# A fifth gate/up weight pair in the storage of a later table: ten f-tiles on token block 0 before block 1 in a fused SSM + GLU kernel

## The chip, the cores and the metric

One core of a Trainium2 chip runs the whole kernel. The metric is the device time of one execution in microseconds (us), read from repeated executions; each ratio compares kernels on one chip, but the chips differ between groups of experiments (1 to 3 with 5; 4 with 6 to 8; 9 and 10; 11 and 12). All comparisons are between executions in the fast state; the only one marked slow (at a granted clock of 0.993) is left out and named where it fell. In experiments 4, 9 and 10 some executions that count as fast have a clock of 0.993 to 0.997; where that matters it is said. A profile is one execution.

Names: PE does the matmuls, DVE and ACT are the vector and scalar engines, POOL is GpSimd and here mostly issues loads, SP (SyncE) issues the transposing transfers. A *token block* is 512 tokens. An *f-tile* is 128 columns of the gate and up weights; a *pair* is the weights of two f-tiles (576 KB). A *slot* is 12 f-tiles on two token blocks, followed by a *down stage*.

## The reference

```python
xn = layernorm(x)                        # x: 1 x 2048 x 576
out = x + A(xn) + B(xn)
def A(x):                                # diagonal complex state-space model, 576 states
    dt = exp(log_dt); Lam_bar = exp(dt * Lam)
    Bu = einsum("bld,pd->blp", x, ((Lam_bar - 1) / Lam)[:, None] * Bmat)
    h[t] = Lam_bar * h[t-1] + Bu[:, t]
    return 2 * einsum("blp,dp->bld", h, Cmat).real + x * Dskip
def B(x):                                # gated MLP, 576 -> 4608 -> 576
    return (sigmoid(x @ w_gate) * (x @ w_up)) @ w_down
```

## The kernel before

The instruction order on every engine is the order of emission. The first loads, all but the first tokens from POOL:

```python
def load_wgu(key, eng_g, eng_u):
    ...
    w = wpool.tile([P, NH, FP * P], BF16, name="wgu", bufs=4)      # four pairs fit
    ...
for pr in range(2):
    load_wgu((0, pr), nc.gpsimd, nc.gpsimd)
for tt in range(TT_B, 2 * TT_B):
    load_x(tt, nc.gpsimd, "hst")
dskip_rows = consts.tile([P, D], BF16, name="dskip_rows")
nc.gpsimd.dma_start(dskip_rows[:], A_Dskip.partition_broadcast(P))
for pr in range(2, 4):
    load_wgu((0, pr), nc.gpsimd, nc.gpsimd)
```

Block 1's tokens are normalised on DVE and transposed by four SP transfers (`xT<-xn`); then DVE adds the skip term for eight token tiles (`ln_resid`, which reads `dskip_rows`). A gate/up group is 18 matmuls, two evictions by ACT (`sT`, `uT`) and one product on DVE (`hT`):

```python
def evac(self):
    ...
    nc.scalar.activation(sT[:], self.ps[:, 0, :], ACT.Sigmoid)
    nc.scalar.copy(uT[:], self.ps[:, 1, :])
    h = hpool.tile([P, TB], BF16, name="hT", bufs=2 * FC)
    nc.vector.tensor_mul(h[:], sT[:], uT[:])
    ...
    bg.step(...)      # gives time credit to queued background work (skip terms, SSM chain)
```

Slot 0's order, and the loads of its down weights:

```python
order = [(f, 0) for f in range(2, 8)] + [(f, 1) for f in range(0, 8)]     # (0,0) and (1,0) come first
order += [(f, nb) for nb in range(2) for f in range(8, 12)]
...
if g.slot == 0:
    if n_used >= 16:
        prefetch_wd(n_pairs)          # six loads of down weights
...
side_loads.extend([load_consts] + bt_loads)     # nine small SSM constants, then transposes of B
```

Of the kernel before, what the change touches and what calls it, by code (L numbers as in the profile page):

```python
# [13 lines left out]
BF16 = mybir.dt.bfloat16  # L14
# [52 lines left out]
def kernel(  # L67
# [17 lines left out]
    nc = tc.nc  # L85
    P = 128
# [8 lines left out]
    TB = 512  # L95
# [7 lines left out]
    NU = PT + 1  # L103
# [3 lines left out]
    NH = D // H  # L107
    FQ = 4
    FP = 2
# [9 lines left out]
    consts = ctx.enter_context(tc.tile_pool(name="consts", bufs=1))  # L119
    wpool = ctx.enter_context(tc.tile_pool(name="wpool", bufs=1))  # L120
# [13 lines left out]
    def load_x(tt, eng, tag=None):  # L134
        if tag is None:
            xt = lnp.tile([P, D], BF16, name="xt", bufs=8)
        else:
            xt = hpool.tile([P, D], BF16, name="xt0", tag=tag, bufs=10)
        eng.dma_start(xt[:], x[tt * P:(tt + 1) * P, :])
        xts[tt] = xt  # L140
# [4 lines left out]

    def load_wgu(key, eng_g, eng_u):
        f0 = (key[0] % NC * (FC // FP) + key[1]) * FP * P
        w = wpool.tile([P, NH, FP * P], BF16, name="wgu", bufs=4)
        fs = slice(f0, f0 + FP * P)
        for (eng, rows, src) in ((eng_g, slice(0, H), B_w_gate), (eng_u, slice(H, P), B_w_up)):  # L150
            eng.dma_start(w[rows, :, :], src[:, fs].rearrange("(c p) f -> p c f", p=H))  # L151
        wgu_t[key] = w
# [12 lines left out]
        load_wgu((0, pr), nc.gpsimd, nc.gpsimd)  # L165
    for tt in range(TT_B, 2 * TT_B):
        load_x(tt, nc.gpsimd, "hst")
    dskip_rows = consts.tile([P, D], BF16, name="dskip_rows")
    nc.gpsimd.dma_start(dskip_rows[:], A_Dskip.partition_broadcast(P))
    for pr in range(2, 4):  # L170
        load_wgu((0, pr), nc.gpsimd, nc.gpsimd)

    eps_t = consts.tile([P, 1], FP32, name="eps_t")
    nc.vector.memset(eps_t[:], 1e-5)
# [132 lines left out]
    qim = consts.tile([P, NU], FP32, name="qim")  # L307
    nqre = consts.tile([P, NU], FP32, name="nqre")
    c512, s512 = sc4[:, 3, :], sc4[:, 2, :]
    T1 = consts.tile([P, NU, TB], BF16, name="T1")  # L310
    T2 = consts.tile([P, NU, TB], BF16, name="T2")
    C2 = consts.tile([P, NU, TB], BF16, name="C2")
    S2 = consts.tile([P, NU, TB], BF16, name="S2")
# [62 lines left out]
        nc.vector.tensor_scalar(s512[:, PT:NU], s512[:, PT:NU], sg_pm[:], -1.0, ALU.mult, ALU.mult)  # L376

    def tables(pt, part):
        sb_, cb_ = sc_tab[(pt, 0)], sc_tab[(pt, 1)]
        col = slice(pt, pt + 1)  # L380
        if part == 0:
            t = ssmp.tile([P, TB], FP32, name="ttab", tag="bure", bufs=2)
            nc.vector.tensor_scalar_mul(t[:], sb_[:], qim[:, col])
            nc.vector.scalar_tensor_tensor(T1[:, pt, :], cb_[:], qre[:, col], t[:], ALU.mult, ALU.add)
            return
        t2 = ssmp.tile([P, TB], FP32, name="ttab2", tag="buim", bufs=2)
        nc.vector.tensor_scalar_mul(t2[:], sb_[:], nqre[:, col])
        if pt < PT:
            nc.vector.scalar_tensor_tensor(T2[:, pt, :], cb_[:], qim[:, col], t2[:], ALU.mult, ALU.add)
            nc.vector.tensor_scalar_mul(C2[:, pt, :], cb_[:], 2.0)  # L390
        else:
            nc.vector.scalar_tensor_tensor(t2[:], cb_[:], qim[:, col], t2[:], ALU.mult, ALU.add)
            nc.vector.tensor_scalar(T2[:, pt, :], t2[:], sg_pm[:], -1.0, ALU.mult, ALU.mult)
            nc.vector.tensor_scalar(C2[:, pt, :], cb_[:], sg_pm[:], 2.0, ALU.mult, ALU.mult)
        nc.vector.tensor_scalar_mul(S2[:, pt, :], sb_[:], -2.0)
# [14 lines left out]
    def ssm_w(nb, pt, part):  # L410
        bre, bim = bu[(nb, pt)]
        t1, t2 = T1[:, pt, :], T2[:, pt, :]
        if part == 0:
# [59 lines left out]
    bg = Background()  # L473
# [63 lines left out]
    def emit(g):  # L537
        g.open()
        g.mms()
        g.evac()  # L540
# [85 lines left out]
    def want_bu(i):  # L626
        if i < len(chain):
            bu_wanted.append(chain[i])
# [25 lines left out]
    n_slots = NSB * NC  # L654
    n_pairs = FC // FP
    all_pairs = [(s, p) for s in range(n_slots) for p in range(n_pairs)]
    wgu_next = [4]
    wd_next = [0]
    pairs_done = [0]

    def prefetch_wgu(n):
        while wgu_next[0] < min(n, len(all_pairs)):
            load_wgu(all_pairs[wgu_next[0]], nc.gpsimd, nc.gpsimd)
            wgu_next[0] += 1

    def prefetch_wd(n):
        while wd_next[0] < min(n, len(all_pairs)):
            load_wd(all_pairs[wd_next[0]])
            wd_next[0] += 1
# [3 lines left out]
    def used(g):  # L673
        if not isinstance(g, GateUp):
            return
        key = (g.slot, g.f // FP)
        uses[key] = uses.get(key, 0) + 1
        if uses[key] == FP * NB_SB:
            pairs_done[0] += 1
            prefetch_wgu(pairs_done[0] + 4)  # L680

        n_used = sum(v for k, v in uses.items() if k[0] == g.slot)
        if g.slot == 0:
            if n_used >= 16:
                prefetch_wd(n_pairs)
        elif n_used % 3 == 0:
            prefetch_wd(g.slot * n_pairs + min(n_used // 3, n_pairs))

    def between_steps():

        if 1 in ssm_done and 1 not in c_done and glu_done[0]:
            for tl in range(TT_B):
                d_step(TT_B + tl, c_terms(1, tl), True)
                acc_free[0] = TT_B + tl + 1
            c_done.add(1)

    def flush_bu():
        if bu_wanted:
            emit(StateIn(*bu_wanted.popleft()))

    def catch_up(nb):

        while nb not in ssm_done:
            flush_bu()
            bg.step(5.0)

    side_loads = deque()

    def run_groups(groups):
        for i, g in enumerate(groups):  # L710
            flush_bu()
            emit(g)
            used(g)
            if side_loads and i % 3 == 2:
                side_loads.popleft()()
            between_steps()

# [68 lines left out]
    for g in start_groups:  # L786
        g.evac()
        used(g)
        bg.step(4.5)

    def catch_up_ln(nb):
        while nb not in ln_done:
            bg.step(5.0)

    for sb in range(NSB):
        b0 = sb * NB_SB
        for c in range(NC):
            slot = sb * NC + c
            if slot == 0:
                order = [(f, 0) for f in range(2, 8)] + [(f, 1) for f in range(0, 8)]  # L800
                order += [(f, nb) for nb in range(2) for f in range(8, 12)]
            else:
                order = [(f, b0 + nbl) for fq in range(0, FC, 4) for nbl in range(NB_SB) for f in range(fq, fq + 4)]
            if slot == 1:
                side_loads.extend(ct_loads)
                for i in range(len(chain)):
                    queue_ssm(i)
                want_bu(0)
                want_bu(1)
            if slot == 2:  # L810
                queue_ln(2, 0)
                queue_ln(2, 1)
            if slot == 0:
                run_groups([GateUp(slot, f, nb) for (f, nb) in order[:6]])
                catch_up_ln(1)
                order = order[6:]
                side_loads.extend([load_consts] + bt_loads)
            run_groups([GateUp(slot, f, nb) for (f, nb) in order])
            if slot == 0:
                split_bt()  # L820
                bg.add(0.0, sines)
                bg.gap()
                bg.add(2.9, per_state_q)
                for pt in range(NU):
                    bg.add(1.2, lambda pt=pt: tables(pt, 0))
                    bg.add(2.1, lambda pt=pt: tables(pt, 1))
            if slot == 2:
                catch_up(0)
                catch_up_ln(2)
                queue_ln(3, 0)  # L830
                queue_ln(2, 2)
                queue_ln(3, 2)
            for tt in range(NB_SB * TT_B):
                nbl, tl = divmod(tt, TT_B)
                nb = b0 + nbl
                final = c == NC - 1 and (nb != 1 or 1 in ssm_done)
                if final:
                    catch_up(nb)
                terms = [(hT[(f, nb)][:, tl * P:(tl + 1) * P], wd_t[(slot, f // FP)][:, f % FP, :]) for f in range(FC)]
                if final:  # L840
                    terms += c_terms(nb, tl)
                d_step(sb * NB_SB * TT_B + tt, terms, final, last=slot == n_slots - 1 and tt == NB_SB * TT_B - 1)
                if slot == 2 and final:
                    acc_free[0] = tt + 1
                if slot == 2 and tt == TT_B - 1:
                    c_done.add(0)
                if slot == 2 and tt == NB_SB * TT_B - 1:
                    glu_done[0] = True
                    if final:
                        c_done.add(1)  # L850
                between_steps()
# [30 lines left out]
```

## Time and profile before

| | before |
|---|---|
| median of the runs given at first | 509.85 us |
| span of the profiled execution | 508.4 us |
| PE busy | 500.6 us |
| block 1's transposes landed (issue of the last plus its time to landing) | 27.4 us |
| first down stage on PE begins | 58.71 us |

The prediction shows the totals, PE's waits and the gap. In the timeline of the kernel before, columns are start, duration, engine, line, operation, tiles, count, and in brackets the idle time before with what ended it.

```profile
7.40 0.54 POOL L169 DMA_DIRECT2D dskip_rows<-in_A_Dskip_dram  x1 [0.67 <-DMA wgu<-in_B_w_gate_dram]
...
58.71 11.57 PE L562 MATMUL pd<-wd,hT 128*128 128x288 bf16 x93
```

The skip row is asked for at 7.40, ahead of pairs 2 and 3, and POOL's issue itself waits for earlier loads. This view is cut at its end; in the prediction's chain all 192 matmuls of the first down stage are one piece.

### The profile page before, as it was taken

To read this page: it belongs to the slowest core of one execution; us is meant where nothing else is said; L and a number is where in the kernel's file an instruction comes from. 1 tells how busy PE (TensorE), PEld (TensorE's weight loads), DVE (VectorE), ACT (ScalarE), POOL (GpSimd) and SP (SyncE) were. 2 spreads that over 40 slices of the span, in tenths; PEclk is the share of its full clock that TensorE was granted. 3 is DMA by queue.
4 is the path that set the end of the run, shared out by engine and by line. 5 is a ranking of instruction groups with operands and counts; after the bars stand their busy time and mean duration, and the time that the engine had idled before them with its cause. 6 is when DMAs were issued, how large, how long until landed. Compare 5 with 4: busy or idle time off the path is not lost.

```text
span 508.4 us, 10667 instructions
## 1 busy us (share of the span) xinstructions
PE 500.6 (98%) x4536; PEld 292.6 (58%) x4536; DVE 323.5 (64%) x703; ACT 204.6 (40%) x368; POOL 96.6 (19%) x143
## 2 busy tenths in 40 slices
PE   8989999999999999999999999999999999999996
PEld 5445676444477444467764444774444774446775
DVE  6964999977888587868688667786675222221111
ACT  4757642556500756530016655005655005553000
POOL 6147430133110043110001231100431001300000
PEclk9999999999999999999999999999999999999999
DMA  8997997075220098342340662200753201600001
GB/s 208 172 170 143 235 194 125 2 164 122 57 57 25 1 170 153 76 107 69 73 104 3 163 141 48 46 24 1 150 122 81 48 25 38 172 1 4 33 25 36
DMA packets 42960, 45.60 MB, mean 90 GB/s; under 512 B 30496, under 2 KB 34336, under 8 KB 42912
## 3 DMA queue, kind: packets, MB, share of 16 engines
q0 software_dynamic: 12672, 34.23, 31.7%
q1 hardware_dynamic: 29808, 10.33, 10.2%
q8 instruction: 35, 0.57, 0.5%
q10 hardware_dynamic: 432, 0.37, 0.2%
q14 instruction: 13, 0.11, 0.1%
HBM read 34.36 MB, written 2.36 MB: 72 GB/s over the span
## 4 chain that ended last, share of the span: by engine, by line
PE 94%; DVE 3%; DMA 1%; ACT 1%; issue 0%
PE pgu L488 52%; PE pd L562 35%; PE pbu L517 7%; DVE bnst L220 1%; DMA xT<-xn 1%; DVE xn L240 1%; DMA xt<-in_A_x_dram 1%; ACT xT L737 0%; DVE acc L263 0%; PE ptr L734 0%; DVE mv L221 0%; DVE tmpxd L260 0%; DVE hT L497 0%; DVE ob L571 0%; DVE xn L245 0%
## 5 line engine op out<-in xcount | busy, mean ns | idle before, releaser
L488 PE MATMUL pgu<-xT,wgu 64*128 64x512 bf16 (+1 forms) x2628 | 283.7, 373 | 1.8 <-DMA xT<-xn 1.8
L488 PEld LDWEIGHTS <-wgu 64*128 64x128 bf16 x2628 | 130.0, 94 | 150.7 <-issue 2.5
L562 PE MATMUL pd<-wd,hT 128*128 128x288 bf16 x1152 | 144.6, 286 | 0.0
L494 ACT ACTIVATE sT<-pgu 128x512 bf16<-128x512 f32 x144 | 86.5, 600 | 119.4 <-PE pgu L488 109.7
L562 PEld LDWEIGHTS <-hT 128*128 128x128 bf16 x1152 | 112.2, 98 | 30.7 <-issue 0.8
L497 DVE TENSOR_TENSOR hT<-sT,uT 128x512 bf16<-128x512 bf16 x144 | 60.5, 421 | 100.0 <-ACT uT L495 99.8
L495 ACT CAST uT<-pgu 128x512 bf16<-128x512 f32 x144 | 84.1, 584 | 0.0
L151 POOL DMA_DIRECT2D wgu<-in_B_w_gate_dram x36 | 27.7, 769 | 227.7 <-PE pgu L488 207.7
L523 ACT COPY bure<-pbu 128x512 f32<-128x512 f32 x16 | 9.4, 585 | 104.3 <-PE pbu L517 88.5
L157 POOL DMA_DIRECT2D wd<-in_B_w_down_dram x36 | 26.4, 735 | 100.6 <-PE pd L562 99.5
L582 DVE TENSOR_TENSOR acc<-acc,pd 128x576 f32<-128x576 f32 x32 | 23.9, 750 | 24.1 <-PE pd L562 24.1
L579 DVE TENSOR_TENSOR ob<-acc,pd 128x576 bf16<-128x576 f32 x15 | 11.3, 754 | 40.9 <-PE pd L562 40.9
L517 PE MATMUL pbu<-xT,bt 64*128 64x512 bf16 x288 | 33.7, 376 | 0.0
L562 PEld LDWEIGHTS <-hst 128*128 128x128 bf16 x288 | 28.2, 98 | 7.1
L151 POOL DMA_DIRECT2D wgu<-in_B_w_up_dram x36 | 26.7, 742 | 1.5 <-issue 0.8
L562 PE MATMUL pd<-ctre,hst 128*128 128x288 bf16 x128 | 26.6, 286 | 0.0
L562 PE MATMUL pd<-ctim,hst 128*128 128x288 bf16 x128 | 26.6, 286 | 0.0
L432 DVE TENSOR_TENSOR_SCAN gre<-r,g0re,wrim 128x512 bf16<-128x512 f32 x20 | 25.5, 1277 | 0.1
L517 PEld LDWEIGHTS <-bt 64*128 64x128 bf16 x288 | 13.7, 94 | 17.1 <-issue 0.9
L439 DVE TENSOR_TENSOR_SCAN gim<-r,g0im,wrim 128x512 bf16<-128x512 f32 x16 | 20.4, 1276 | 0.0
L220 DVE BATCH_NORM_STATS2 bnst<-xt 128x6 f32<-128x288 bf16 x32 | 12.5, 433 | 2.4 <-DMA xt<-in_A_x_dram 2.4
L419 DVE TENSOR_TENSOR tq<-T,buim 128x512 bf16<-128x512 bf16 x20 | 13.7, 684 | 0.0
(113 smaller groups left out, 273.9 us busy)
## 6 DMA issues: line engine op xcount, KB each, us to landing
wgu<-in_B_w_gate_dram POOLq DMA_DIRECT2D x36, 288.0 KB, 4.4
wgu<-in_B_w_up_dram POOLq DMA_DIRECT2D x36, 288.0 KB, 5.1
wd<-in_B_w_down_dram POOLq DMA_DIRECT2D x36, 288.0 KB, 6.2
out_dram<-ob SPq DMA_DIRECT2D x15, 144.0 KB, 1.8
xt<-in_A_x_dram SPq DMA_DIRECT2D x10, 144.0 KB, 2.6
xt<-in_A_x_dram POOLq DMA_DIRECT2D x4, 144.0 KB, 7.2
bt<-ctre POOLq DMA_DIRECT2D x2, 288.0 KB, 6.9
bt<-ctim POOLq DMA_DIRECT2D x2, 288.0 KB, 7.8
```

Of the source, the lines that this page charges most:

```text
L151: eng.dma_start(w[rows, :, :], src[:, fs].rearrange("(c p) f -> p c f", p=H))
L157: nc.gpsimd.dma_start(wd[:], B_w_down[f0:f0 + FP * P, :].rearrange("(n p) d -> p n d", p=P))
L220: nc.vector.bn_stats(st[:, gi, :], xt[:, gi * DH:(gi + 1) * DH])
L432: nc.vector.tensor_tensor_scan(gre[:], r_bc, w[:, 0, :], g0re[:, col], ALU.mult, ALU.add)
L439: nc.vector.tensor_tensor_scan(gim[:], r_bc, w[:, 1, :], g0im[:, col], ALU.mult, ALU.add)
L488: nc.tensor.matmul(self.ps[:, gi, cols], w[rows, c, fs], xT[self.nb][rows, c, cols], start=c == 0, stop=c == NH - 1)
L494: nc.scalar.activation(sT[:], self.ps[:, 0, :], ACT.Sigmoid)
L495: nc.scalar.copy(uT[:], self.ps[:, 1, :])
L497: nc.vector.tensor_mul(h[:], sT[:], uT[:])
L517: nc.tensor.matmul(out, w, xT[self.nb][rows, c, ts_], start=c == 0, stop=c == NH - 1)
L562: nc.tensor.matmul(out, lhsT, rhs[:, a * DH:(a + 1) * DH], start=i == 0, stop=i == n - 1)
L582: nc.vector.tensor_add(halves(acc[:]), halves(acc[:]), pd[:, :, 0:DH])
```

## The change

The intent is that PE works on block 0 until block 1's transposed tokens are there. A fifth pair is loaded early, into storage that the first SSM table (`T1`) needs only later, and the order becomes ten f-tiles on block 0, ten on block 1, then the last two on each.

```diff
-        w = wpool.tile([P, NH, FP * P], BF16, name="wgu", bufs=4)
+        if key == (0, 4):
+            w = consts.tile([P, NH, FP * P], BF16, name="wgu4", tag="T1")
+        else:
+            w = wpool.tile([P, NH, FP * P], BF16, name="wgu", bufs=4)
 ...
+    for pr in range(2, 4):
+        load_wgu((0, pr), nc.gpsimd, nc.gpsimd)
     dskip_rows = consts.tile([P, D], BF16, name="dskip_rows")
     nc.gpsimd.dma_start(dskip_rows[:], A_Dskip.partition_broadcast(P))
-    for pr in range(2, 4):
-        load_wgu((0, pr), nc.gpsimd, nc.gpsimd)
+    load_wgu((0, 4), nc.gpsimd, nc.gpsimd)
 ...   (T1 itself is allocated at its first use)
-    wgu_next = [4]
+    wgu_next = [5]
-            prefetch_wgu(pairs_done[0] + 4)
+            prefetch_wgu(max(pairs_done[0] + 4, min(pairs_done[0], 4) + 5))
-            if side_loads and i % 3 == 2:
+            if side_loads and i % 3 == 1:
-                order = [(f, 0) for f in range(2, 8)] + [(f, 1) for f in range(0, 8)]
-                order += [(f, nb) for nb in range(2) for f in range(8, 12)]
+                order = [(f, 0) for f in range(2, 10)] + [(f, 1) for f in range(0, 10)]
+                order += [(f, nb) for nb in range(2) for f in range(10, 12)]
 ...   (slot 1)
+                bg.add(0.0, lambda: want_bu(0))
+                bg.add(0.0, lambda: want_bu(1))
                 for i in range(len(chain)):
                     queue_ssm(i)
-                want_bu(0)
-                want_bu(1)
 ...   (slot 0: the first run of groups is order[:8] instead of order[:6])
```

More of the change, by code (lines that the diff above doesn't have):

```diff
@@ L309 @@
     c512, s512 = sc4[:, 3, :], sc4[:, 2, :]
-    T1 = consts.tile([P, NU, TB], BF16, name="T1")
+    T1 = None
     T2 = consts.tile([P, NU, TB], BF16, name="T2")
@@ L378, in tables @@
     def tables(pt, part):
+        nonlocal T1
+        if T1 is None:
+            T1 = consts.tile([P, NU, TB], BF16, name="T1", tag="T1")
         sb_, cb_ = sc_tab[(pt, 0)], sc_tab[(pt, 1)]
@@ L813 @@
             if slot == 0:
-                run_groups([GateUp(slot, f, nb) for (f, nb) in order[:6]])
+                run_groups([GateUp(slot, f, nb) for (f, nb) in order[:8]])
                 catch_up_ln(1)
-                order = order[6:]
+                order = order[8:]
                 side_loads.extend([load_consts] + bt_loads)
```

## The prediction

> **What bounds the kernel now.** I read the page's engine totals first, then PE's own waits, then the chain in order of time, and last the timeline around the one gap that those views leave.
>
> ```profile
> span 508.4 us, 10667 instructions
> PE 500.6 (98%) x4536; PEld 292.6 (58%) x4536; DVE 323.5 (64%) x703; ACT 204.6 (40%) x368; POOL 96.6 (19%) x143
> ...
> PEclk9999999999999999999999999999999999999999
> ```
>
> PE is busy for 500.6 of 508.4 us at an undiminished clock, so at most 7.8 us could go without removing matmul work. The waits of PE tell which of it is a wait:
>
> ```profile
> PE pgu L488 <- DMA xT<-xn: 1.8, 1, 1.8
> PE pgu L726 <- DVE warm L178: 1.3, 1, 1.3
> PE ptr L734 <- DVE xn L245: 0.7, 1, 0.7
> ```
>
> Three waits, each once: 1.8 + 1.3 + 0.7 = 3.8 us. The other 4.0 us is the tail: in the chain PE ends at 504.47 and the last eviction and output transfer run to 508.4. The 1.3 and the 0.7 lie in the first 7 us, which the change does not touch. The 1.8 is what it aims at. In the chain in order of time:
>
> ```profile
> 22.80 0.27 DVE tmpxd L260
> 23.07 4.31 DMA xT<-xn
> 27.38 0.14 issue
> 27.52 31.26 PE pgu L488 x288
> 58.77 23.63 PE pd L562 x192
> 82.40 2.05 PE pbu L517 x18
> 84.45 1.94 PE pgu L488 x18
> ```
>
> The reader is to see that up to 27.38 the end depends on a transfer, the last of the four transposes that make the normalised tokens of block 1; from 27.52 on the chain is PE alone until the tail. So PE waits once for block 1, and never again. The timeline gives both sides of the gap:
>
> ```profile
> 10.95 14.78 PE L488 MATMUL pgu<-xT,wgu 64*128 64x256 bf16 x162
> ...
> 17.83 6.60 SPq L256 DMA_TRANSPOSE xT<-xn  x4
> ...
> 27.52 31.26 PE L488 MATMUL pgu<-xT,wgu 64*128 64x512 bf16 x288 [1.79 <-DMA xT<-xn]
> ```
>
> Eight f-tiles on block 0 are done at 10.95 + 14.78 = 25.73; the next is block 1's; PE stands still for 27.52 - 25.73 = 1.79 us.
>
> **What the Trainium skill says.** "Perfetto Trace Analysis", section "Identifying the Most-Contended Engine", warns that matmul busy share is not a good measure of the distance from roofline. So I checked the pace: 31.26 us / 288 = 108.5 ns a matmul of K = 64 and 512 columns. "TensorE: Matmul & The Clock Gate", section "Part 3: Packing small matmuls — row/col tiling", says matmuls with K under 128 on different row groups run concurrently; the trace agrees, since one such matmul lasts 373 ns in the page and they still start every 108.5 ns. Its section "Back-to-back issue gap" gives 518 cycles at 2.4 GHz for 512 columns, 216 ns, or 108 ns each for two side by side (estimate from that page): the stream is at its pace, and no hidden stall in it is there to win. "DMA: Bandwidth & Descriptors", section "Issuing engines are not separate DMA queues", says that transfers of all issuers share the same 16 DMA engines and interleave. That bears on the added early load, which is queued by POOL while SP's transposes run. The profile before shows the engines near full in most slices up to 28 us, and whether interleaving slows the transposes no run has shown yet.
>
> **The change part by part.**
>
> 1. The order in slot 0: f-tiles 0 to 9 on block 0 (before, 0 to 7), then 0 to 9 on block 1. Two f-tiles move ahead of the wait: 2 x 18 matmuls x 108 ns = 3.88 us. Block 0 then ends at 25.73 + 3.88 = 29.61, and the block 1 transposes landed at 27.38. There is 29.61 - 27.38 = 2.2 us of slack, so the whole wait goes if the transposes slip by less. Gain: 1.79 us. The matmuls are the same ones; nothing is added to PE.
>
> 2. Their weights, pair 4, must be there at 25.73. Before, four pairs fit and pair 4 was issued at 31.88, once pair 0 was free. Now it has a buffer of its own and goes out right behind dskip. POOL's issues of pairs 2 and 3 ran from 8.86 to 13.3, with dskip ahead of them at 7.40. I place the two new issues, 0.75 us each, at about 13.1 to 14.6. What they wait for is the queue: it was drained by about 18.3 (in the stretch 18 to 19 it moved 0.05 MB). Pair 4 is 576 KB, at the 198 GB/s of 14 to 16 us some 2.9 us. So it lands at about 21.2, or 22.5 if it shares evenly with the transposes: 3 us early. The same sum moves dskip behind pairs 2 and 3, to about 18.3; its first reader starts at 20.39.
>
> 3. What the load costs the transposes. From 18.1 to 22 the DMA engines have about 2 us of idle time (shares of 0.34, 0.62 and 0.69 in three of those stretches). Of 2.9 us of load 0.8 us is left that displaces transposes. I take a slip of about 1 us, to 28.4, inside the slack of 2.2 us. Residual wait: 0, or some tenths of a microsecond.
>
> 4. T1's storage: the first table now waits until pair 4's last reader on block 1 is done, about 29.61 + 10 x 1.94 = 49. Before, DVE wrote its first table at 71.69. No wait.
>
> 5. The state inputs of slot 1 are asked for in the background queue behind the tables, instead of at once. The instruction order on PE shows four gate/up tiles between the first down stage and the first state input, where there was none; the counts per stage are equal, except that one state input moves from before the second slot-2 down stage boundary to after it. Before, ACT stood 0.32 and 1.46 us in front of state-input evictions until tables on DVE freed their buffers. That stops, but PE never waited there, so it is worth 0.
>
> 6. Weights prefetched one pair later and side loads one group earlier: pair 5 leaves when pair 0 is done at 29.61 + 3.88 = 33.5, needed at 49. Worth 0.
>
> Sum: -1.79 on the path, 0 to +0.5 for a residue. 509.85 - 1.75 = **508.1 us**, a third of a per cent.
>
> **Rivals.**
>
> - The wait comes back as a wait for weights or for slipped transposes. For it: the DMA engines are near full, and the skill's interleaving. Against: 3 and 2.2 us of slack. If transposes slip by 4 us, the residue is 1.8 and the time stays at 509.8.
> - The evictions become the bound. Around 24 us ACT waited 2.38 us for DVE, which worked through the residual sums, before evicting an f-tile. For PE that would be a new wait if a PSUM slot were late. The ninth f-tile starts at 25.73 and takes the slot of the fifth, whose eviction began at 20.86 and was over by about 22; the tenth takes that of the sixth, evicted from 24.39 to 25.5, needed at 27.67. So it is 2 us early: unlikely.
> - The later state inputs delay the scans until a down stage waits for them. Before, the last state of block 1 was written at about 228, and its first reader came at 246: 18 us of slack against a shift of two f-tiles, 3.9 us. At the end DVE is 20% busy. It would take an unforeseen pile-up to reach PE; then 1 to 3 us more than before.
> - An unseen gain, from ACT no longer blocked: PE has no second wait to lose, so nothing beyond 1.8.
>
> **Range and chances.** The central time takes the whole wait. Below it there is only the scatter of runs (509.46 to 509.96 before), above it there are a partial slip and the rivals. Range 507.4 to 509.7. Faster by over 2% would need 10.2 us, more than all idle time of PE: 0.01. Slower by over 2% would need a new stall that nothing in the profile announces: 0.01. Within 2%: 0.98.
>
> **What would show it.** In the profile after, PE's list of waits lacks the one for block 1's transposes, or has it below 0.5; the first gate/up stretch runs unbroken from 10.95 to about 57; PE busy stays at 500.6 +- 0.5 while the span falls to about 506.6. The first POOL loads show five pairs; the transposes land by 29. The prediction is wrong if PE shows a new wait, on weights near 25.7, on evictions near 28 to 33 or 85 to 100, or on states near 220 to 260, or if the matmuls' pace drops below what it was.

## More of the kernel before

A down stage sums, for each of 8 token tiles, twelve `hT` tiles times `wd` in two halves of 288 columns: 24 matmuls, in the order of f. So the 23rd matmul of the first token tile is the first to read f-tile 11, and the 21st the first to read the last down weights.

## The result, and the profile after

The changed kernel took 509.32 us (median of 6, 508.32 to 509.86), the kernel before 509.89 us (6 runs, 509.46 to 510.0) on the same chip. The ratio is 0.999, 95% interval 0.9977 to 1.0003: the same. Ratios here are the mean time of one kernel's fast runs over that of the other's of the same rounds, so not quite the ratio of the medians.

So the class was right and the time lies in the range, but of the 1.75 us expected only 0.6 us shows in the medians. The profiled execution was the fastest of the six (508.32). Its totals, PE's waits and its timeline:

```profile
span 506.5 us, 10662 instructions
...
PE 500.9 (99%) x4536; PEld 290.1 (57%) x4536; DVE 324.1 (64%) x703; ACT 204.9 (40%) x368; POOL 96.9 (19%) x143
```

```profile
PE pgu L733 <- DVE warm L182: 1.3, 1, 1.3
PE pd L569 <- DVE hT L504: 0.4, 1, 0.4
PE ptr L741 <- DVE xn L249: 0.3, 1, 0.3
```

```profile
10.69 45.86 PE L495 MATMUL pgu<-xT,wgu 64*128 64x256 bf16 x450
56.48 2.87 PE L569 MATMUL pd<-wd,hT 128*128 128x288 bf16 x22
59.70 10.46 PE L569 MATMUL pd<-wd,hT 128*128 128x288 bf16 x84 [0.35 <-DVE hT L504]
...
11.78 0.58 POOL L174 DMA_DIRECT2D dskip_rows<-in_A_Dskip_dram  x1
...
17.60 7.33 SPq L260 DMA_TRANSPOSE xT<-xn  x4
```

The wait for `xT` is gone and the gate/up stretch is one unbroken piece of 45.86 us, as intended. But there is a wait that was not there before: after 22 matmuls of the first down stage PE stands 0.35 us for `hT`, the product of f-tile 11 of block 0. And SP now needs 7.33 us for the four transposes that took 6.60. This execution lost little; its neighbours at 509.1 to 509.9 lost more, and were not profiled. Where did their 1 us go?

### The profile page after: what moved, and what is told of

It is laid out like the page before. It is cut to its first block, busy times and chain, and to the rows that moved or that the text cites. A ratio compares the mean times of both kernels' runs of the same rounds, so it can differ in the third digit from the quotient of the medians.

```text
span 506.5 us, 10662 instructions
## 1 busy us (share of the span) xinstructions
PE 500.9 (99%) x4536; PEld 290.1 (57%) x4536; DVE 324.1 (64%) x703; ACT 204.9 (40%) x368; POOL 96.9 (19%) x143
## 4 chain that ended last, share of the span: by engine, by line
PE 94%; DVE 3%; ACT 1%; DMA 1%; issue 0%
PE pgu L495 52%; PE pd L569 34%; PE pbu L524 7%; DVE sctab L325 1%; DVE rnd L324 1%; DMA xt<-in_A_x_dram 1%; DVE ang L349 1%; PE ptr L741 0%; DVE hT L504 0%; ACT xT L744 0%; DVE bnst L224 0%; ACT L328 0%; ACT uT L502 0%; ACT L501 0%; ACT sT L501 0%
## 5 line engine op out<-in xcount | busy, mean ns | idle before, releaser
L495 PEld LDWEIGHTS <-wgu 64*128 64x128 bf16 x2628 | 127.6, 94 | 151.1 <-issue 0.5
L154 POOL DMA_DIRECT2D wgu<-in_B_w_gate_dram x36 | 27.9, 776 | 227.2 <-PE pgu L495 208.2
```

The costliest lines, as they stand in the source:

```text
L154: eng.dma_start(w[rows, :, :], src[:, fs].rearrange("(c p) f -> p c f", p=H))
L495: nc.tensor.matmul(self.ps[:, gi, cols], w[rows, c, fs], xT[self.nb][rows, c, cols], start=c == 0, stop=c == NH - 1)
```

## The experiments

Two theories, and a rival to both. The expectations speak of them by letter or in words.

- **A, the late tail.** The new order completes block 0 only two f-tiles (2 x 1.94 = 3.9 us) before its down stage, where it was four. PE also gets there 2 us sooner. PE then waits for DVE's product, or for the last down weights.
- **B, the slip.** The early 576 KB delay block 1's transposes, and the skip row behind pairs 2 and 3, by more than the 1 us predicted; slack and gain are eaten there.
- **Rival.** The state inputs moved into the background queue cost or gain something, or the difference is scatter.

### 1. The changed kernel again

No edit, five timed rounds.

> The changed kernel once more, unedited, to see which waits of PE another execution has. The trace of its fastest execution showed a full gain of 1.9 us in the span, the six executions together only 0.6 us in the median. Theory A (the tail of slot 0): the first down stage now waits for the last block 0 tile's product on DVE, 0.35 us in the fast trace, and more in others: the trace shows that wait at 0.3 to 1.6 us and the time is 509.0 to 509.7. Theory B (slipped transposes): the wait for block 1's transposes is back in other executions, up to 1.5 us. Theory C: no new wait, the six runs were scatter: time 508.1 to 508.6.

Measured: 508.81 us (508.42 to 510.66), ratio 0.9986 (0.9973 to 0.9999). So there is a gain, of 0.7 us by the ratio (0.0014 x 510), and the interval (0.05 to 1.4 us) holds neither 0 nor the 1.75 expected: scatter alone is not the answer. PE's wait beyond those of its start, the piece of its chain for the last down weights, and the transposes:

```profile
PE pd L569 <- DMA wd<-in_B_w_down_dram: 0.5, 1, 0.5
```

```profile
50.48 9.85 DMA wd<-in_B_w_down_dram
```

```profile
57.21 2.62 PE L569 MATMUL pd<-wd,hT 128*128 128x288 bf16 x20
60.36 9.84 PE L569 MATMUL pd<-wd,hT 128*128 128x288 bf16 x79 [0.53 <-DMA wd<-in_B_w_down_dram]
...
18.25 8.29 SPq L260 DMA_TRANSPOSE xT<-xn  x4
21.45 0.46 DVE L264 TENSOR_TENSOR tmpxd<-xn,dskip_rows 128x576 bf16<-128x576 bf16 x1 [0.56 <-DMA dskip_rows<-in_A_Dskip_dram]
```

Here the down stage stops after 20 matmuls, so for the last weights (asked for at 50.48, on the path until 60.3) and not for the product. The transposes landed at 29.8, 2.4 us later than before, just inside PE's end of block 0 (30.0, since PE's long stretch began at 11.34 instead of 10.95). The skip row came too late for DVE. Both theories are visible, each with a small wait.

### 2. Only the state inputs moved

```diff
# kernel before
+                bg.add(0.0, lambda: want_bu(0))
+                bg.add(0.0, lambda: want_bu(1))
-                want_bu(0)
-                want_bu(1)
```

> The kernel before with one part of the change alone: the first two state inputs are asked for in the background queue behind the tables. The prediction calls it worth 0: within 0.3 us of before. If the later state inputs cost PE something (theory D), 0.5 to 1.5 us slower, with a new wait of PE beyond 80 us.

Measured: 509.94 us (509.6 to 510.46), ratio 1.0003 (0.999 to 1.0016), with PE's wait for `xT` still at 1.6 us. On the kernel before, this part is worth between -0.5 and +0.8 us by the interval, and its centre is 0: the rival that puts the missing 1 us there falls.

### 3. The late tail alone

```diff
# kernel before
-                order += [(f, nb) for nb in range(2) for f in range(8, 12)]
+                order += [(f, nb) for fq in (8, 10) for nb in range(2) for f in range(fq, fq + 2)]
```

> The kernel before with only the tail of slot 0 as in the change: tiles 8 and 9 on both blocks, then 10 and 11 on both, so that block 0 is complete two tiles before the down stage. Theory A: PE waits for DVE's product at the start of the first down stage, 0.3 to 1.5 us, time 510.2 to 511.2. Theories B and C: as before, within 0.3 us.

Measured: 510.66 us (509.42 to 510.69), ratio 1.0012 (1.0 to 1.0024). The timeline at the first down stage:

```profile
58.31 3.02 PE L562 MATMUL pd<-wd,hT 128*128 128x288 bf16 x22
...
61.49 0.42 DVE L497 TENSOR_TENSOR hT<-sT,uT 128x512 bf16<-128x512 bf16 x1
...
61.96 2.26 PE L562 MATMUL pd<-wd,hT 128*128 128x288 bf16 x17 [0.63 <-DVE hT L497]
```

The kernel before, with nothing but the new tail, gets the new wait: 22 matmuls, then 0.63 us for the product, which DVE reaches at 61.49. That is theory A: the wait belongs to the order of the tail, and is there with no early pair, and with PE arriving only 0.4 us sooner (58.31 for 58.71). (The last down weights landed at 60.9 in this profile, about when PE came to them; in the kernel before at 58.3.)

### 4. The early load alone

```diff
# kernel before
+    extra = consts.tile([P, NH, FP * P], BF16, name="extra", tag="T1")
+    for (rows, src) in ((slice(0, H), B_w_gate), (slice(H, P), B_w_up)):
+        nc.gpsimd.dma_start(extra[rows, :, :], ...)     # pair 4's columns, read by nobody
```

> The kernel before with pair 4's weights loaded once more, at the place of the change, into storage that nothing reads; the order of tiles is unchanged, so PE's wait for block 1's transposes shows their slip in full. The prediction's slip of 1 us: wait 2.8 us, time 510.9. Theory B, a slip of 2 to 3 us as the traces of k1 and k2 suggest: wait 3.8 to 4.8 us, time 511.9 to 512.9. No slip: wait 1.8, time 509.9.

Measured: 513.4 us (509.97 to 514.87, 4 runs), ratio 1.0046 (1.0013 to 1.0078). The order of work is that of before, so PE shows the slip openly:

```profile
11.37 15.19 PE L494 MATMUL pgu<-xT,wgu 64*128 64x256 bf16 x162
30.45 32.94 PE L494 MATMUL pgu<-xT,wgu 64*128 64x512 bf16 x288 [3.89 <-DMA xT<-xn]
...
18.28 8.99 SPq L259 DMA_TRANSPOSE xT<-xn  x4
```

The wait is 3.89 us instead of 1.79, and the transposes landed at 30.3 instead of 27.4: a slip of 2.9 us with the same 576 KB. Not all of it need be the load's: by 14 us, when the extra load is only being issued, POOL's queue had moved 2.13 MB instead of 2.27. Nor is it in every execution: one of the four took 509.97 us, as the kernel before. The total rose by more than the wait, because the 288 matmuls behind it took 32.94 instead of 31.26 us: the granted clock in that stretch was 0.95. So I take the slip from this run, not the total. That is theory B. What the two transfer queues moved from 19 to 20 us shows how it comes about, first in the kernel before, then in experiment 1, which has the early pair (q0 is POOL's queue, q1 SP's; packets, MB, share of the engines):

```profile
q1 hardware_dynamic: 512, 0.13, 166.5%
q0 software_dynamic: 3, 0.00, 0.8%
```

```profile
q0 software_dynamic: 73, 0.22, 92.5%
q1 hardware_dynamic: 15, 0.00, 2.1%
```

While POOL's queue is full, SP's transposes hardly move: the first of them, issued at 17.83 and 18.25, landed after 4.7 us before and after 6.8 us in experiment 1. Before, that queue had moved 99% of its early bytes by 18.2; in experiments 1 and 4 to 8 by 21.2 to 22.0, and in the fast first profile already by 19.6.

### 5. The tail earlier

```diff
# changed kernel
-                order = [...] + [(f, 1) for f in range(0, 10)]
-                order += [(f, nb) for nb in range(2) for f in range(10, 12)]
+                order = [...] + [(f, 1) for f in range(0, 8)]
+                order += [(10, 0), (11, 0)] + [(f, 1) for f in range(8, 12)]
```

> The changed kernel with f-tiles 10 and 11 of block 0 moved ahead of tiles 8 and 9 of block 1, so that block 0 is complete four tiles before the down stage, as in the kernel before, instead of two. Theory A: the wait for DVE's product is gone, 508.0 us (507.6 to 508.4), about 1 us faster than the changed kernel. Theory B (transposes) and C (scatter): same time as the changed kernel of this job, within 0.3 us.

Measured: 508.79 us (507.62 to 509.98; a sixth execution, 517.31, was slow), ratio 0.9978 (0.9964 to 0.9993). The wait at the down stage is gone; PE's list has another, and DVE's has a longer one for the skip row:

```profile
PE pgu L495 <- DMA wgu<-in_B_w_up_dram: 1.0, 1, 1.0
```

```profile
DVE tmpxd L264 <- DMA dskip_rows<-in_A_Dskip_dram: 1.7, 1, 1.7
```

Pair 2, issued at 8.71, took 10.2 us to land in this execution, and the transposes landed at 30.6. Theory A's part is mended, since the wait for the product is gone, but the median is that of the changed kernel of the same job (508.81), not the 1 us less that A expected; in this profile the crowded front takes 1.0 us.

### 6 and 7. Down weights sooner, with and without the earlier tail

```diff
-            if n_used >= 16:
+            if n_used >= 13:
```

Together with the earlier tail:

> The changed kernel with both late waits taken away: tiles 10 and 11 of block 0 moved ahead (as in k2), and the six down weights issued right behind the SSM constants, ahead of pairs 6 and 7, so some 3 us earlier. Theory A+E (the change uncovers DVE's products and the down weights at the first down stage): no wait of PE at the first down matmuls, median 508.0 (507.6 to 508.5). If the early transfers (theory B) take the rest, PE shows a wait before 31 us and the median stays at 508.6 to 509.2.

Measured: 508.88 us (508.11 to 509.29), ratio 0.9974 (0.9962 to 0.9986). No wait at the down stage, 0.5 us for `xT` (landed at 30.6) and 0.2 for weights.

Alone on the changed kernel:

> The changed kernel with only the down weights issued sooner. Theory E (down weights): no wait of PE for them, but DVE's product is still waited for, 0.3 to 1 us; median 508.3 to 508.8. If the down weights never mattered but in one execution, same as the changed kernel, 508.8 to 509.3.

Measured: 510.0 us (509.67 to 512.49), ratio 1.0009 (0.9991 to 1.0027). PE's waits that are new against before:

```profile
PE pd L569 <- DVE hT L504: 1.4, 1, 1.4
...
PE pgu L495 <- ACT uT L502: 0.6, 1, 0.6
```

With the late tail left in, sooner weights only hand the wait to the product, here 1.4 us. The 0.6 us is an eviction: the skip row held DVE until 22.02, DVE then ran three skip tiles before the next product, and ACT, whose buffers that product frees, stood 4.07 us. This is the same front as in the changed kernel, so it shows what its slower executions may hold; I did not catch one of those in a profile.

### 8. One more look at the changed kernel

> One more look at the changed kernel, for another execution's waits. Theory B: block 1's transposes land 1.5 to 3 us later than in the kernel before (29 to 30.5 us). Theories A and E: a wait of 0.3 to 1 us before the first down matmuls, for DVE's product or for the down weights.

Measured: 509.2 us, one execution (its state is unknown, as for any single run). PE waited 0.5 us for the last down weights and 0.2 us for `xT`, which landed at 29.8; the skip row made DVE wait 1.7 us.

| profile | transposes landed | new waits of PE, up to the first down stage |
|---|---|---|
| before, and experiments 2 and 3 (no early pair) | 27.4, 27.2, 27.0 | wait for `xT` 1.8, 1.6, 1.2; experiment 3 also `hT` 0.6 |
| changed (first profile) | 27.5 | `hT` 0.4 |
| changed, experiments 1 and 8 | 29.8, 29.8 | `wd` 0.5; `wd` 0.5 and `xT` 0.2 |
| same loads, experiments 5, 6, 7 | 30.6, 30.6, 30.0 | 1.0; 0.7; 2.0 |
| before with the extra load, experiment 4 | 30.3 | `xT` 3.9 |

Experiments 1 and 2 ran on the same chip, so the 29.8 against 27.2 is not a difference of chips.

### 9 and 10. The skip row behind the transposes

If the front is too full, take something out of it. The skip row goes out on SP behind block 1's transposes, and the skip terms wait until block 1's groups have begun. On top of experiment 6, and then on top of experiment 5:

```diff
-    nc.gpsimd.dma_start(dskip_rows[:], A_Dskip.partition_broadcast(P))
 ...   (background queue, behind block 1's transposes)
+    bg.add(0.0, lambda: nc.sync.dma_start(dskip_rows[:], A_Dskip.partition_broadcast(P)))
-    bg.add(0.0, bg.owe)              # had set the time credit to -2 ahead of the skip terms
-        bg.add(1.25, lambda tt=tt: ln_resid(tt))
+        bg.add(1.25, lambda tt=tt: ln_resid(tt), ready=lambda: resid_go[0])   # set once block 1 has begun
```

> The kernel k5 (tail of block 0 early, down weights sooner) with the crowd of early transfers thinned: the broadcast of Dskip leaves the weight queue and follows block 1's transposes on SP, and the residual sums that read it run on DVE once block 1 has begun. Theory B (crowding of the first 30 us): the transposes land 0.5 to 1 us sooner than in k5 (29.3 to 30.0 instead of 30.9), DVE no longer waits for Dskip at 22 us, no PE wait near 30 us; median 507.9 to 508.5, faster than before by 0.3 to 0.4 per cent. If crowding is not what is left, as k5: 508.9.

> The same as k9 but with the down weights where the change has them. If the down weights are late only in some executions, 0.2 to 0.5 us slower than k9 and a PE wait for down weights of up to 0.5 us; if they don't matter once the tail is moved, the same as k9 within 0.3 us.

Measured: 510.66 us (510.36 to 512.93), ratio 1.0028 (1.0006 to 1.0049), and 512.86 us (510.35 to 516.16), ratio 1.0057 (1.0025 to 1.0088): slower than before, a miss. Five of these twelve executions had a clock of 0.995 to 0.997, and they are among the longest; but the rest too took 510.35 us or more, against a median of 509.89 before. PE's longest wait in the first:

```profile
PE pd L568 <- DVE hst L471: 2.0, 1, 2.0
```

The front did what it should: transposes at 27.6, no wait of PE between its start and the third slot's down stage. But the state chain came later: block 1's last state was written at about 255 us, in the changed kernel at about 226, and PE stood 2.0 us for it. My reading of the code is that the skip terms used up the credit that the chain draws on; experiment 11 bears it out. The second also waited 0.9 us for weights and 1.8 us for an eviction, before which ACT had stood 5.34 us for the small constant `ldt`: the third thing that experiment 11 finds.

### 11. Skip terms paced, tail three tiles early

```diff
# experiment 9
-        bg.add(1.25, ..., ready=lambda: resid_go[0])
+        bg.add(0.9, ..., ready=lambda tt=tt: bg.now >= 11 + max(0, tt - 1))    # about one a tile
-                order = [...] + [(f, 1) for f in range(0, 8)]
-                order += [(10, 0), (11, 0)] + [(f, 1) for f in range(8, 12)]
+                order = [...] + [(f, 1) for f in range(0, 9)]
+                order += [(10, 0), (11, 0)] + [(f, 1) for f in range(9, 12)]
```

> The changed kernel with its three weak spots mended together: the dskip load issued on SyncE behind block 1's transposes, the residual steps that read it paced one per tile instead of in one burst (so the state chain keeps its place in VectorE's order), block 0's last two tiles pulled three tiles ahead of the first down stage, and six down weights issued right behind the state constants. Theory (the removed 1.8 us of waiting was eaten by the slip of the transposes and dskip, and by the product or last down weight at the first down stage): slot 0 has no TensorE wait after its start, block 1's transposes land at 27.5 to 28.5 us, no wait for hT or wd, and the median is 507.9 to 508.6 with a ratio of 0.995 to 0.9975. Rival (the gain is bounded by something that a cleaner slot 0 can't reach, the state chain or scatter of the clock): the median stays at 508.8 to 509.5, or a wait of about 2 us for hst comes back in slot 2 and it is 510 or more.

Measured: 508.86 us (507.94 to 512.03), ratio 0.9977 (0.9958 to 0.9997), just above the range expected. Four executions took 507.94 to 509.1, two 511.05 and 512.03, all at a clock of 1.0. The profile fell on the slowest. PE's waits, and ACT's timeline:

```profile
PE pgu L494 <- ACT uT L501: 2.2, 1, 2.2
PE pd L568 <- DVE hT L503: 1.3, 1, 1.3
```

```profile
41.90 0.58 ACT L501 CAST uT<-pgu 128x512 bf16<-128x512 f32 x1
46.93 1.28 ACT L327 ACT_TABLE_LOAD   x1 [4.46 <-DMA ldt<-in_A_log_dt_dram]
```

The wait for `hst` is gone, so pacing kept the state chain in place. What is left is a third thing: the small constant `ldt` (2 KB) took 11.0 us to land, right behind pair 5's up weights, which went out ahead of it on POOL's queue at 34.63 and took 11.4 us, in a stretch where the transposes of B were under way (one of them took 14.6 us). ACT stood 4.46 us for it with the next eviction behind it in its order.

### 12. The constants asked for at the start

```diff
# experiment 11
+    load_consts()                     # right behind pair 4, at about 14 us
-                side_loads.extend([load_consts] + bt_loads)
+                side_loads.extend([mark_consts] + bt_loads)   # only the place in the order is kept
```

> The run before it (dskip behind the transposes, paced residuals, tail three tiles early, down weights sooner) with one more edit: the nine small loads of SSM constants are issued right behind pair 4 at about 15 us, not in slot 0 behind pair 5. In that run two of six executions took 511 to 512 us, and the profiled one shows ldt landing at 46.9, ScalarE standing 4.5 us for it in front of an eviction, and TensorE waiting 2.2 us for that eviction and 1.3 us for hT. Theory (the late constants made those two executions): ldt lands by 28 us, ScalarE has no wait for it, TensorE has no wait between its start and 100 us, no execution is over 510 and the median is 507.9 to 508.6 (ratio 0.9955 to 0.997). Rival (a slow transfer hits whatever is asked for late, here pair 5 or the transposes): ldt is early, but a wait of 1 us or more for weights, transposes or products is still there in some executions, and the median stays at 508.6 to 509.3.

Measured: 508.13 us (507.96 to 508.44, 6 runs), the kernel before 510.13 us (12 runs, eleven of them those of experiment 11, on the same chip), ratio 0.996 (0.9948 to 0.9972). It is the fastest version of all, and the steadiest: its six executions lie within 0.5 us, those of experiment 11 on the same chip within 4.1. PE's whole list of waits, then its timeline, with SP's transposes, and ACT's:

```profile
PE pgu L736 <- DVE warm L181: 1.3, 1, 1.3
PE ptr L744 <- DVE xn L252: 0.7, 1, 0.7
```

```profile
10.88 46.18 PE L498 MATMUL pgu<-xT,wgu 64*128 64x256 bf16 x450
56.99 23.70 PE L572 MATMUL pd<-wd,hT 128*128 128x288 bf16 x192
...
17.80 7.97 SPq L263 DMA_TRANSPOSE xT<-xn  x4
```

```profile
42.65 1.28 ACT L331 ACT_TABLE_LOAD   x1
```

These are the waits of the kernel before, 1.3 and 0.7 in the first 7 us, without the 1.8 and with nothing in its place; the down stage runs its 192 matmuls in one piece. The transposes landed at 27.9. ACT goes to its table load with no wait on a transfer, 0.02 us after the eviction before it. What this run does not separate: early constants also take nine issues out of POOL's order in slot 0, which lets later weights go out sooner, and I did not put the early constants on the changed kernel alone.

## Why the prediction was right or wrong

**Right: class, bound, and the gain that was there.** PE is the bound, and its wait for block 1 was worth 1.8 us. Experiment 12 has PE's waits exactly as the prediction's first part would leave them, and takes 508.13 us, where 508.1 was predicted; the profiled spans differ by 508.4 - 506.6 = 1.8 us, the medians by 510.13 - 508.13 = 2.0 us, against 1.75. But that is a kernel with several more edits. For the change itself the time fell in the range only because the range reached up to 509.7: of the gain, 0.6 to 0.7 us came.

**The pace: right, by weaker grounds than it says.** Durations that overlap don't show that matmuls of K = 64 run side by side: those of the down stage have K = 128, last 286 ns and still start every 23.69 us / 192 = 123 ns. What shows it is that 512 columns start every 108.5 ns, half of the 219 ns that the down stage's 288 columns in 123.4 ns scale to (estimate from the trace). The section on the back-to-back issue gap also calls its 216 ns that of a single matmul and gives about 131 ns for a stream, which the prediction left out; this trace sides with the 216.

**Step 1, the order: right.** The wait for `xT` went, or shrank to 0.2 us.

**Step 2, pair 4 and the skip row: half right.** No profile of the changed kernel shows a wait for pair 4. The skip row was put at 18.3, ahead of its reader at 20.39; it landed at 20.3 in the first profile, just in time, and in experiments 1 and 8 its reader got it at 21.45 and 22.1, with DVE waiting 0.6 and 1.7 us. The step took the time when the queue goes quiet for the landing: in the kernel before, the queue was quiet at 18.3, but its last load, issued at 12.58, landed 8.0 us later, at 20.6.

**Step 3 failed in its size.** It said "I take a slip of about 1 us, to 28.4, inside the slack of 2.2 us." Measured: 0.1 us in the first profile, 2.4 us in each of the two others, 2.9 us in experiment 4. The mechanism was the one named, a load that displaces transposes; what failed is the room it was given. The estimate set 2 us of idle time of the DMA engines between 18 and 22 us against the 2.9 us of load. The three shares that it quotes leave only 0.66 + 0.38 + 0.31 = 1.35 us, the stretch it skips, 19 to 20, was at 1.67, and little of it was left once the load was there: the transposes hardly moved until POOL's queue ran low, as the lines of experiment 4 show. The small slip of the first profile is luck of that execution: its loads ran faster from the start, POOL's queue had moved 2.38 MB by 14 us, where the kernel before had 2.27 and experiments 1 and 8 had 2.21 and 2.26. The slack just covered the rest: PE waited 0, 0 and 0.2 us for `xT` in the three profiles, in experiment 1 only because PE itself was 0.4 us late. The sign "the transposes land by 29" failed in two of three. What the same load did to the skip row, two steps further on, is not in that step at all.

**The sum lacked a term.** It ended at "0 to +0.5 for a residue", and no rival looked at the first down stage. The order that hides the transposes also makes block 0 complete two f-tiles before that stage instead of four, while PE gets there 1.5 to 2.2 us sooner. All three profiles of the changed kernel wait there: 0.35 us for the product, 0.53 and 0.47 us for the last down weights. Experiment 3 shows that the order of the tail alone is enough for the wait for the product; experiments 5 and 6 that with four tiles of distance it is gone. For the down weights the distance is not shown to matter: they were asked for no sooner than before (the last at 49.65 before, 50.48 and 50.55 in experiments 1 and 8), and PE came sooner. In experiment 5 they landed 1.3 us earlier than in experiment 1 and PE came 0.8 us later, in experiment 6 they were asked for sooner.

**Steps 4 and 5 hold.** No table waited for storage, and the state inputs moved alone gave 1.0003. Step 6, the later prefetch and earlier side loads, is not tested: no run took them alone.

**Where the 1.1 us went.** The profiles of experiments 1 and 8 (509.12 and 509.2 us) lost it by the end of the first down stage: PE goes on to the next work at 81.53 and 81.55, where it was 82.33 before and 80.64 in the first profile. So 0.8 us was gained of 1.8. Of the missing 1.0 us the new waits are 0.53 and 0.70; in experiment 1 PE's long stretch also began 0.4 us later than before, with the loads of the first 11 us, and in experiment 8 it ran 0.3 us longer over block 0. (It began at 10.69 in the first profile, at 10.95 before: part of that profile's 1.9 us is luck.) Which of these fill the slower executions without a profile stays open. Experiment 7, with the same front, shows what else can be there (an eviction behind the late skip row, a product 1.4 us late), and experiment 12 that a kernel with front, tail and constants mended together has the whole gain.

**The rivals.** Slipped transposes were real, 2.4 to 3.2 us in all profiles but one, short of the 4 us that would have cost everything. The eviction rival was seen in experiment 7 (0.6 us). The scan rival was absent from the changed kernel and came with my own edit in experiments 9 and 10, at the size it named, 1 to 3 us.

## What to carry to other kernels

When a reorder takes PE off one wait, read the next hand-over downstream as well: count how many tiles lie between the last producer and its first reader, before and after. An early load is not free because its consumer has slack; what it does to the transfers issued beside it was, in all profiles but one, two to three times what idle shares suggested here, and adding the load alone, unread, measures it. The time at which a queue goes quiet is not the time at which its last load has landed. Small loads that an in-order engine reads should be asked for long before they are read: in experiment 12 `ldt` still took 8.6 us, but nobody stood for it.

## What the Trainium skill lacked or had wrong

- "DMA: Bandwidth & Descriptors", section "Issuing engines are not separate DMA queues", says that transfers of all issuers interleave; it gives no size for what they do to each other. Here, with one more load of 576 KB from GpSimd, issued some 4 to 5 us ahead of the first of four SyncE transposes, the last of them landed 2.4 to 3.2 us later in six of seven profiles and 0.1 us later in one; from 19 to 20 us in experiment 1 the transposes moved 0.00 MB beside GpSimd's 0.22.
- "DMA: Bandwidth & Descriptors", section "Anatomy of one DMA — SWDGE (gpsimd) path", gives a fixed cost of about 2.0 us for a GpSimd load plus its bytes. In this case's traffic the 2 KB load of `ldt` took 4.3 to 8.6 us in most profiles, and 11.0 and 11.8 us in two. That section has no figure for a queue that is loaded.
- I found no page that says that GpSimd's issuing waits for its own earlier loads once several are outstanding. Here the ninth load stood until the first had landed, and so on: some 0.5 to 1.2 us ahead of most of the early weight issues, and 6.42 us in experiment 11. Whether the chip or the program's own semaphores make it wait, no run here shows.
